# A fixed four-slot table for the feed-forward of a top-k attention kernel

## The chip, the core and the metric

The kernel runs on one core of one Trainium2 chip. The metric is device time in microseconds. The core has TensorE (PE, with its weight loads shown apart as PEld), VectorE (DVE), ScalarE (ACT), GpSimd (POOL) and SyncE (SP). Each takes its instructions in program order and waits where an operand or a buffer is not ready.

## The reference

Attention over 8 batches, 8 heads, 576 positions and 64 dimensions, in which a query keeps its 32 highest scores; then a feed-forward layer with a cosine gate. All in float32.

```python
scores = scale * np.matmul(q, k.transpose(0, 1, 3, 2))
kth = np.partition(scores, -top_k, axis=-1)[..., -top_k:-top_k + 1]
scores = np.where(scores >= kth, scores, -1e9)
scores = scores - np.max(scores, axis=-1, keepdims=True)
attn = np.exp(scores)
attn = attn / (np.sum(attn, axis=-1, keepdims=True) + 1e-09)
x = np.matmul(attn, v)          # to (4608 tokens, 512)
h = x @ w_in                    # 512 -> 2048
return (h * np.cos(h)) @ w_out  # 2048 -> 512
```

The second line from the end is why a product is gated with a sine: cos(h) is the sine of an argument that was first brought into range.

## The kernel before

**Units, slots, blocks.** The 4608 tokens are cut into 36 blocks of 128. A unit is 128 tokens with a pair of heads, so a block has four units and there are 144. One slot (`slot`, called for i = 0 to 143) handles three units at once at three stages: the top-k search of unit i, the mask and exponentials of unit i - 1, and the transfer of unit i - 2 through DRAM, which transposes its probabilities into a ring of five places. Four slots make a round and carry one block's worth of everything. Slots are named below by i modulo 4.

**Attention.** PE makes the scores of two units in every even slot (`scores`, L242). ACT copies them out (`take_scores`, L253 and L257). DVE folds 576 scores into two halves (L267) and takes the 32 highest with alternating MAX8 and MATCH_REPLACE8 (L359, L364); POOL makes the lower half `low` (`fold_sum` L283, `fold_low` L292), which DVE needs only in the last search round. A slot begins, on DVE, with the merge of the unit before (L347, L352); ACT then masks it (L378) and takes exponentials (L387). POOL splits the probabilities into 16-bit halves (L410) with their reciprocal sums (L412), and SP writes and transposes them. In every slot with i modulo 4 equal to 2, PE multiplies a block's probabilities by V (`values`, L475, into the PSUM tile `rim`), and DVE scales the result into `xT` (`take_values`, L491 or L499).

**Feed-forward.** A block's first product (`ff1`, L553) is made in four groups, each filling one PSUM bank of 128x512: mm0 to mm3 in this text. For each bank ACT makes two reads, `g` (L567) and `x` (L569, with a conversion to integers, `take_first`). For each pair of banks, 128x1024, POOL makes the argument in two operations (`reduce_first` L589, `reduce_second` L598), ACT takes the sine (L608, after a table load, and another load before the next exponentials), POOL multiplies (`gate`, L615). The second product (`ff2`, L628) runs over 16 slices; four make a group, o(0) to o(3), all in one bank, which ACT empties and stores (`take_second`, L638). The two banks of tag `mm` serve mm and o alike.

**The order.** Attention's order is written out in `slot`. The feed-forward is fed in by a planner: `plan` names for each slot of a round how many items of the two products are wanted at two or three places, and `can_first` and `can_second` decide by counters (gated tiles, ticks, loaded weights) whether an item may go. Filled banks wait in a list that `take_banks` empties; arguments, sines and gates go through queues. After the last slot `drain` and `forward` finish by the same queues with arguments and gates on DVE. q, k and v are loaded by SP inside `send`, at slots chosen by `load_at`. In the first twelve slots the weights are decoded by ACT, DVE and POOL between all this.

Of the kernel before, what the change touches and what calls it, by code (L numbers as in the profile page):

```python
# [17 lines left out]
P = 128  # L18
# [12 lines left out]
def kernel(  # L31
# [64 lines left out]
    ff = {"live": 0, "tick": 0, "now": 0, "end": False, "kind": 0, "half": 0, "open": 0, "late": False}  # L96
# [213 lines left out]
    def topk_first(u, w):  # L310

        u["top"] = tops[u["n"] % len(tops)]
        if w:
            merge_first(w)
        if u["n"] not in BUSY:
            fold_sum(u)
        fold_high(u)
        if w:
            merge_second(w)
        if u["n"] in BUSY:  # L320
            fold_now(u)
        topk_round(u, 0, [lambda: distances(w), lambda: None] if w else ())
# [82 lines left out]
    def split(u):  # L405


        s = u.pop("s").rearrange("p j k -> p (j k)").bitcast(U16)
        halves = work.tile([P, 2, 2 * S + P], U16, tag="halves", name="halves", bufs=1)
        nc.gpsimd.tensor_copy(out=halves[:, :, 0 : 2 * S], in_=s.rearrange("p (k h) -> p h k", h=2))  # L410
        rden = u.pop("rden").bitcast(U16).rearrange("p (j h) -> p h j", h=2)
        nc.gpsimd.tensor_copy(  # L412
            out=halves[:, :, 2 * S :].rearrange("p h (j d) -> p h j d", j=2),
            in_=rden.unsqueeze(3).to_broadcast([P, 2, 2, D]),
        )
        u["halves"] = halves
# [64 lines left out]
    def take_values(us):  # L481
# [23 lines left out]
        blk["left"] -= n  # L505
        blk["tick"] = ff["tick"]


    widths = [P] * (B * S // P)
    blocks, block_of = [], {}  # L510
    t0 = 0
    for w in widths:
        blk = {"t0": t0, "w": w, "left": 0, "g": [], "gated": []}
        for u in units:
            if t0 <= u["tok"] < t0 + w:
                block_of[u["tok"]] = blk
                blk["left"] += 1
        blocks.append(blk)
        t0 += w


    first = deque((blk, i) for blk in blocks for i in range(2 * NF * blk["w"] // 512))
    second = deque(
        (blk, i, f) for blk in blocks for i in range(blk["w"] // P) for f in range(0, NF, 2)
    )
    fresh = deque()
    waiting = deque()
    sined = deque()
    full = deque()

    def open_bank():

        if ff["open"] + len(full) == 2:
            take_banks()
        ff["open"] += 1

    def ff1(blk, i):
        w = blk["w"]
        nf = 256 // w
        part = i % 4  # L540
        if part == 0:
            blk["g"].append(ffw.tile([P, 1024], F32, tag="g", name="g", bufs=CHUNKS))
            blk["x"] = ffw.tile([P, 1024], F32, tag="x", name="x", bufs=XB)
            ff["live"] += 1
        if part % 2 == 0:
            open_bank()
            blk["mm"] = ps.tile([P, 512], F32, tag="mm", name="mm", bufs=2)
        g, mm = blk["g"][-1], blk["mm"]
        for a in range(nf):
            f = i * nf + a  # L550
            at = (part % 2 * nf + a) * w
            for c in range(NC):
                nc.tensor.matmul(  # L553
                    mm[:, at : at + w],
# [5 lines left out]
        if part % 2 == 0:  # L560
            return
        ff["open"] -= 1
        full.append((take_first, blk, g, blk["x"], mm, part // 2))

    def take_first(blk, g, x, mm, half):
        at = slice(half * 512, half * 512 + 512)
        nc.scalar.mul(out=g[:, at], in_=mm, mul=INV_2PI / UP)  # L567

        nc.scalar.activation(  # L569
            out=x[:, at].bitcast(I32), in_=mm, func=AF.Identity, bias=quarter, scale=INV_2PI / UP  # L570
        )
        if half == 1:
            fresh.append([blk, g, x, False, ff["now"] if ff["late"] else 0])

    def take_banks():
        while full:
            take, *what = full.popleft()
            take(*what)

    def reduce_first():  # L580

        if not fresh or (ff["late"] and not ff["end"] and fresh[0][4] == ff["now"]):
            return
        g, x = fresh[0][1:3]
        fresh[0][3] = True
# [5 lines left out]
        )  # L591

    def reduce_second():
        if not fresh or not fresh[0][3]:
            return
        blk, g, x, *_ = fresh.popleft()
        if not ff["end"]:
            nc.gpsimd.tensor_tensor(out=x, in0=g, in1=x, op=ALU.subtract)  # L598
        waiting.append((blk, g, x, ff["now"]))

    def sines(least):

        n = sum(c[3] < ff["now"] for c in waiting)
        if n == 0 or (n < least and waiting[0][3] + 2 > ff["now"]):
            return
        for _ in range(n):
            blk, g, x, _ = waiting.popleft()
            nc.scalar.activation(out=x, in_=x, func=AF.Sin, bias=halfpi, scale=TWO_PI_BELOW)  # L608
            sined.append((blk, g, x))

    def gate(n):
        for _ in range(min(n, len(sined))):
            blk, g, x = sined.popleft()
            eng = nc.vector if ff["end"] else nc.gpsimd
            eng.tensor_tensor(out=g, in0=g, in1=x, op=ALU.mult)  # L615
            blk["gated"].append(ff["tick"])

    def ff2(blk, i, f0):
        w = blk["w"]
        if f0 == 0:  # L620
            open_bank()
            blk["o"] = ps.tile([P, 512], F32, tag="mm", name="o2", bufs=2)
        o = blk["o"]
        per = 1024 // w
        for f in range(f0, f0 + 2):
            g = blk["g"][f // per]
            at = (f % per) * w + i * P
            nc.tensor.matmul(  # L628
                o, g[:, at : at + P], w_out[f], start=f == 0, stop=f == NF - 1
            )  # L630
        if f0 + 2 < NF:
            return
        ff["open"] -= 1
        full.append((take_second, blk, i, o))

    def take_second(blk, i, o):
        ob = ffw.tile([P, DM], F32, tag="ob", name="ob", bufs=1)
        nc.scalar.mul(out=ob, in_=o, mul=2.0 * math.pi / UP)  # L638
        row = blk["t0"] + i * P
        nc.scalar.dma_start(out=out[row : row + P, :], in_=ob)  # L640
        if i == blk["w"] // P - 1:
            ff["live"] -= len(blk["g"])
            blk["g"] = []

    def can_first():
        if not first:
            return False
        blk, i = first[0]
        if blk["left"] or ff["tick"] < blk["tick"] + 2 or wq["ready"] < (((i + 1) * (256 // blk["w"]) - 1) // FC + 1) * NC:
            return False  # L650
        return ff["now"] > NP + 2 and (i % 4 > 0 or ff["live"] + staged() < CHUNKS)

    def can_second():
        if not second or ff["now"] < 2 * NP + 3:
            return False
        blk, i, f = second[0]

        lag = 3 if ff["now"] < NU - NP else 2
        gated = sum(ff["tick"] >= t + lag for t in blk["gated"])
        return gated * 1024 // blk["w"] >= f + 2 and wq["ready"] >= NC * NF // FC + f + 2  # L660

    def item(kind):
        if not (can_first, can_second)[kind]():
            return False
        if kind == 0:
            ff1(*first.popleft())
        else:
            ff2(*second.popleft())
        return True

    def feed(*kinds):

        ff["tick"] += 1
        for kind in kinds:
            item(kind)

    def feed_any(n):

        ff["tick"] += 1
        for _ in range(n):  # L680
            kinds = (ff["kind"], 1 - ff["kind"])
            if second and second[0][2] == 0:
                kinds = (0, 1)
            if item(kinds[0]):
                kind = kinds[0]
            elif item(kinds[1]):
                kind = kinds[1]
            else:
                return
            if kind != ff["kind"] or ff["half"]:  # L690
                ff["kind"], ff["half"] = 1 - kind, 0
            else:
                ff["half"] = 1
# [19 lines left out]
    def load_at(i, *what):  # L713
        while i in at_slot or (what[0] is load_v and i % NP == 0):
# [23 lines left out]
    def send(x):  # L738

        split(x)  # L740
# [5 lines left out]
    plan = (  # L746
        ((0, 0), (1,), (1,)),
        ((0, 0), (1, 1), (0,)),
        ((0,), (1,), ()),
        ((1, 0, 0), (1, 1), ()),  # L750
    )

    def slot(i, u, w, x, z):
        n = (3, 4, 3, 4, 4, 3)[i] if i < NP + 2 else 2 if i != 2 * NP + 1 else 0
        if i < NP:
            for load, b, hp in at_once[i]:
                load(b, hp)
# [3 lines left out]
        ff["late"] = False  # L761
        topk_first(u, w)
# [18 lines left out]

        if i % 2:
            sines(1)
        if w:
            mask(w)
        if i % NP != 3:
# [114 lines left out]
```

## Time and profile before

| | us |
|---|---|
| median of 3 runs | 1413.0 (1412.85 to 1414.05) |
| profiled execution: span | 1410.6 |
| around that span, to the median | 2.4 |
| PE busy | 1354.6 (96%) |
| weight loads busy | 977.2 (69%) |
| DVE busy | 1336.9 (95%) |
| ACT busy | 1140.9 (81%) |
| POOL busy | 1165.3 (83%) |

The span runs from the first to the last instruction of the profiled execution; the runs time the whole execution. In an order of time each row gives the start in the span, the duration, the engine, the line, the operation and its tiles, and in brackets how long the engine had idled and what released it. In a table of groups the numbers behind the bar are the busy time in us, the mean in ns, and the idle time before. In a table of stretches the columns are sum and mean of the stretch, then busy time and count of PE, PEld, DVE, ACT and POOL, the granted TensorE clock, the share of the DMA engines, and GB/s. Durations of neighbours overlap a little, since operations are pipelined; the step from one start to the next is what a queue feels.

### The profile page before, as it was taken

To read this page: it belongs to the slowest core of one execution; us is meant where nothing else is said; L and a number is where in the kernel's file an instruction comes from. 1 tells how busy PE (TensorE), PEld (TensorE's weight loads), DVE (VectorE), ACT (ScalarE), POOL (GpSimd) and SP (SyncE) were. 2 spreads that over 40 slices of the span, in tenths; PEclk is the share of its full clock that TensorE was granted. 3 is DMA by queue.
4 is the path that set the end of the run, shared out by engine and by line. 5 is a ranking of instruction groups with operands and counts; after the bars stand their busy time and mean duration, and the time that the engine had idled before them with its cause. 6 is when DMAs were issued, how large, how long until landed. Compare 5 with 4: busy or idle time off the path is not lost.

```text
span 1410.6 us, 32284 instructions
## 1 busy us (share of the span) xinstructions
PE 1354.6 (96%) x11264; PEld 977.2 (69%) x11264; DVE 1336.9 (95%) x5004; ACT 1140.9 (81%) x2043; POOL 1165.3 (83%) x804
## 2 busy tenths in 40 slices
PE   5558999999999999999999999999999999999998
PEld 3445777777777777777777777777777777777775
DVE  7999999999999999999999999999999999999931
ACT  7887888888888888888888888888888888888831
POOL 4778988888888888888888888888888888898810
PEclk6788999999999999999999999999999999999999
DMA  9566776867675576668666576666766566655540
GB/s 291 193 196 181 204 178 169 203 172 196 162 177 152 161 199 159 181 160 197 174 170 159 152 181 187 170 170 160 207 165 165 158 174 166 148 157 146 152 101 15
DMA packets 427442, 240.12 MB, mean 170 GB/s; under 512 B 375952, under 2 KB 392592, under 8 KB 427280
## 3 DMA queue, kind: packets, MB, share of 16 engines
q1 hardware_dynamic: 420720, 224.22, 61.3%
q10 hardware_dynamic: 6560, 13.85, 2.8%
q8 instruction: 88, 1.44, 0.4%
q14 instruction: 74, 0.61, 0.1%
HBM read 45.09 MB, written 101.19 MB: 104 GB/s over the span
## 4 chain that ended last, share of the span: by engine, by line
PE 91%; DVE 7%; ACT 1%; DMA 0%; POOL 0%; issue 0%; SPq 0%; POOLq 0%
PE o L628 36%; PE mm L553 35%; PE rim L475 10%; PE sc L242 8%; DVE top L359 3%; PE rim L242 2%; DVE rest L364 2%; DVE low L364 1%; DVE rest L267 1%; DVE w_out L151 0%; DVE w_in L151 0%; DMA st<-in_moe_w_in_dram 0%; PE warm L844 0%; DVE low L275 0%; ACT s L387 0%; ACT s L378 0%
## 5 line engine op out<-in xcount | busy, mean ns | idle before, releaser
L553 PEld LDWEIGHTS mm<-xT,w_in 128*128 128x128 f32 x4608 | 537.9, 192 | 70.4 <-issue 65.5
L553 PE MATMUL mm<-xT,w_in 128*128 128x128 f32 x4608 | 539.2, 275 | 2.4 <-DVE xT L491 1.7
L628 PE MATMUL o<-w_out,g 128*128 128x512 f32 x1152 | 524.7, 599 | 0.0
L359 DVE MAX8 top<-rest 128x8 f32<-128x288 f32 x1152 | 479.0, 451 | 0.0
L364 DVE MATCH_REPLACE8 rest<-top,rest 128x288 f32<-128x288 f32 x864 | 376.7, 444 | 0.0
L628 PEld LDWEIGHTS o<-w_out,g 128*128 128x128 f32 x1152 | 207.7, 190 | 219.5 <-issue 214.8
L410 POOL COPY halves<-s 128x2304 uint16<-128x2304 uint16 x140 | 294.9, 2107 | 43.3 <-ACT s L387 40.1
L378 ACT ACTIVATE s<-s,top 128x576 f32<-128x576 f32 x288 | 207.6, 768 | 111.1 <-DVE top L352 99.0
L359 DVE MAX8 top<-low 128x8 f32<-128x288 f32 x576 | 241.8, 449 | 0.4 <-POOL low L292 0.4
L387 ACT ACTIVATE s<-s,nd 128x576 f32<-128x576 f32 x288 | 220.4, 769 | 1.1
L292 POOL TENSOR_TENSOR low<-low,rest 128x576 int32<-128x576 int32 x141 | 199.3, 1413 | 11.0
L283 POOL TENSOR_TENSOR low<-s 128x576 int32<-128x576 int32 x141 | 199.6, 1415 | 6.4 <-ACT s L259 6.4
L598 POOL TENSOR_TENSOR x<-g,x 128x1024 f32<-128x1024 f32 x68 | 161.2, 2370 | 5.7
L242 PE MATMUL sc<-k,q 64*64 64x448 f32 (+1 forms) x1120 | 145.6, 564 | 16.2 <-DVE low L275 9.8
L615 POOL TENSOR_TENSOR g<-g,x 128x1024 f32<-128x1024 f32 x68 | 161.0, 2367 | 0.0
L257 ACT COPY s<-rim 64x256 f32<-64x256 f32 (+1 forms) x280 | 103.1, 368 | 61.6 <-PE rim L475 60.0
L475 PE MATMUL rim<-ring,v 128*64 128x128 f32 (+1 forms) x2560 | 139.0, 268 | 0.0
L475 PEld LDWEIGHTS rim<-ring,v 128*64 128x64 f32 x2560 | 130.0, 139 | 6.5 <-issue 5.7
L253 ACT COPY s<-sc 128x896 f32<-128x896 f32 (+1 forms) x144 | 128.4, 892 | 3.3 <-PE sc L242 3.2
L567 ACT ACTIVATE g<-mm 128x512 f32<-128x512 f32 x144 | 85.2, 592 | 56.5 <-PE mm L553 55.5
L364 DVE MATCH_REPLACE8 low<-top,low 128x288 f32<-128x288 f32 x288 | 125.4, 443 | 0.0
L267 DVE TENSOR_TENSOR rest<-sc,s 128x576 f32<-128x576 f32 x144 | 107.7, 748 | 7.1 <-ACT s L259 6.6
(55 smaller groups left out, 1155.7 us busy)
## 6 DMA issues: line engine op xcount, KB each, us to landing
rows<-halves SPq DMA_DIRECT2D x140, 640.0 KB, 3.5
out_dram<-ob ACTq DMA_DIRECT2D x36, 256.0 KB, 2.1
q<-in_q_dram SPq DMA_DIRECT2D x31, 288.0 KB, 4.4
st<-in_moe_w_in_dram SPq DMA_DIRECT2D x16, 512.0 KB, 5.8
v<-in_v_dram SPq DMA_DIRECT2D x32, 256.0 KB, 4.2
k<-in_k_dram SPq DMA_DIRECT2D x31, 144.0 KB, 4.2
k<-in_k_dram SPq DMA_DIRECT2D x32, 128.0 KB, 4.5
st<-in_moe_w_out_dram SPq DMA_DIRECT2D x8, 512.0 KB, 5.1
```

The source lines that it names most:

```text
L242: nc.tensor.matmul(to[r0 : r0 + rows, rim_bank(r0, j) if k0 else place(u["hp"], j), 0 : k1 - k0], st["q"][d, q0 : q0 + rows], st["k"][d, k ...
L283: nc.gpsimd.tensor_tensor(out=u["low"].bitcast(I32), in0=s[:, :, 0:HS], in1=s[:, :, HS:S], op=ALU.add)
L292: nc.gpsimd.tensor_tensor(out=low, in0=low, in1=u["rest"][:, :, HS:S].bitcast(I32), op=ALU.subtract)
L359: nc.vector.max(to[:, j], src[:, j])
L364: nc.vector.match_replace(rest[:, j], to[:, j], src[:, j], NEG)
L378: nc.scalar.activation(out=s[:, j], in_=s[:, j], func=AF.Prelu, bias=less[:, j], scale=1.0, alpha=FAR)
L387: nc.scalar.activation(out=s[:, j], in_=s[:, j], func=AF.Exp, bias=nd[:, j : j + 1], scale=SCALE, accum_out=den[:, j, 0:1],)
L410: nc.gpsimd.tensor_copy(out=halves[:, :, 0 : 2 * S], in_=s.rearrange("p (k h) -> p h k", h=2))
L475: nc.tensor.matmul(to[d, r], lhsT, rhs, start=(bank, j) not in begun, stop=c == NT - 1 and u in us[-2:] and r0 + rows == P,)
L553: nc.tensor.matmul(mm[:, at : at + w], w_in[f // FC][:, c, (f % FC) * P : (f % FC + 1) * P], blk["xT"][:, c], start=c == 0, stop=c == NC - 1,)
L598: nc.gpsimd.tensor_tensor(out=x, in0=g, in1=x, op=ALU.subtract)
L628: nc.tensor.matmul(o, g[:, at : at + P], w_out[f], start=f == 0, stop=f == NF - 1)
```

## The change

The planner goes, with its counters and queues. `slot` names every feed-forward step for each of the four slots of a round, with the block counted as b = (i - 6) // 4. The groups keep their sizes. In program order a block's steps are: P@V and, at the end of slot 2, mm0; in slot 3, after the score copies, the reads of mm0, then mm1; in slot 0 the reads of mm1 between mask and exponentials, mm2, and at the end the first sine and the reads of mm2; in slot 1 mm3 and then o(0), which used to follow the next block's P@V and now stands ahead of it; o(1), o(2), o(3) in the following slots 2, 3 and 1. The store of a block stands in slot 1 between mask and exponentials.

Arguments and gates are made per bank, 128x512, and not per pair of banks: twelve POOL operations for a block and not six. They stand at named places, some of them ahead of `fold_sum` in a slot (`topk_first` takes a list for that). The sine stays at 128x1024. `split` becomes two functions that are called one after the other. `load_at` now keeps every load out of slots divisible by four, and so out of the sends of slot 1; before it kept only v out. `drain` is written out as one fixed list.

```diff
@@ -307,11 +307,13 @@
-    def topk_first(u, w):
+    def topk_first(u, w, ahead=()):
         u["top"] = tops[u["n"] % len(tops)]
         if w:
             merge_first(w)
+        for step in ahead:
+            step()
         if u["n"] not in BUSY:
             fold_sum(u)
         fold_high(u)
@@ -402,18 +404,21 @@
     def both(u):
         return [lambda: sums(u), lambda: reciprocal(u)] if u else ()
-    def split(u):
+    def split_scores(u):
         s = u.pop("s").rearrange("p j k -> p (j k)").bitcast(U16)
-        halves = work.tile([P, 2, 2 * S + P], U16, tag="halves", name="halves", bufs=1)
+        halves = u["halves"] = work.tile([P, 2, 2 * S + P], U16, tag="halves", name="halves", bufs=1)
         nc.gpsimd.tensor_copy(out=halves[:, :, 0 : 2 * S], in_=s.rearrange("p (k h) -> p h k", h=2))
+    def split_sums(u):
+        halves = u["halves"]
         rden = u.pop("rden").bitcast(U16).rearrange("p (j h) -> p h j", h=2)
         nc.gpsimd.tensor_copy(
             out=halves[:, :, 2 * S :].rearrange("p h (j d) -> p h j d", j=2),
             in_=rden.unsqueeze(3).to_broadcast([P, 2, 2, D]),
         )
-        u["halves"] = halves
...
+    def half_of(tiles, k):
+        return tiles[k // 2][:, k % 2 * 512 : k % 2 * 512 + 512]
...
+    def argument(b, k):
+        blk = block(b)
+        if blk is None:
+            return
+        g, x = half_of(blk["g"], k), half_of(blk["x"], k)
         if ff["end"]:
             nc.vector.tensor_tensor(out=x, in0=g, in1=x.bitcast(I32), op=ALU.subtract)
             return
         nc.gpsimd.tensor_scalar(
             out=x, in0=x.bitcast(I32), scalar1=1.0, scalar2=0.0, op0=ALU.mult, op1=ALU.add
         )
...
+        nc.gpsimd.tensor_tensor(out=x, in0=g, in1=x, op=ALU.subtract)
+    def sine(b, t):
+        blk = block(b)
+        if blk is None:
+            return
+        x = blk["x"][t]
+        nc.scalar.activation(out=x, in_=x, func=AF.Sin, bias=halfpi, scale=TWO_PI_BELOW)
+    def gate(b, k):
+        blk = block(b)
+        if blk is None:
+            return
+        g, x = half_of(blk["g"], k), half_of(blk["x"], k)
+        eng = nc.vector if ff["end"] else nc.gpsimd
+        eng.tensor_tensor(out=g, in0=g, in1=x, op=ALU.mult)
+    def second_run(b, r):
...
+        for f in range(r * PER, (r + 1) * PER):
+            g = half_of(blk["g"], f // PER)
...
@@ -711,7 +635,7 @@
     at_slot, at_once = {}, {}
     def load_at(i, *what):
-        while i in at_slot or (what[0] is load_v and i % NP == 0):
+        while i in at_slot or i % NP == 0:
             i += 1
         at_slot[i] = what
...
     def slot(i, u, w, x, z):
+        m, b = i % NP, (i - NP - 2) // NP
         n = (3, 4, 3, 4, 4, 3)[i] if i < NP + 2 else 2 if i != 2 * NP + 1 else 0
         if i < NP:
-            for load, b, hp in at_once[i]:
-                load(b, hp)
+            for load, bb, hp in at_once[i]:
+                load(bb, hp)
         load_weights(n, nc.sync if i < NP + 2 else nc.scalar)
         if x:
             (turn if i < NP + 2 else send)(x)
-        ff["late"] = False
-        topk_first(u, w)
+        if m == 1:
+            gate(b, 0)
+        elif m == 0:
+            argument(b, 0)
+        topk_first(u, w, [lambda: argument(b - 1, 3)] if m == 2 else ())
         fold_low(u)
         topk_round(u, 1)
         topk_round(u, 2)
         if i > 1:
             decode_second(NP)
             decode_third()
-        reduce_first()
-        reduce_second()
-        made = scored.get(i, [])
-        if z:
-            take_banks()
-        feed(*((0, 0) if i == NP + 2 else plan[i % NP][0]))
-        for m in made:
-            scores(m)
+        for o in scored.get(i, []):
+            scores(o)
         if z:
             values(z)
-        if i % 2:
-            sines(1)
+        if m == 1:
+            gate(b, 1)
+            argument(b, 2)
+            second_run(b - 1, 3)
+        elif m == 2:
+            second_run(b - 1, 1)
+        elif m == 3:
+            second_run(b - 1, 2)
         if w:
             mask(w)
-        if i % NP != 3:
-            take_banks()
+        if m == 0:
+            take_first(b, 1)
+            argument(b, 1)
+            first_bank(b, 2)
+        elif m == 1:
+            take_second(b - 1)
+            first_bank(b, 3)
+            second_run(b, 0)
         if w:
             exponentials(w)
-        take_banks()
+        if m == 2:
+            sine(b - 1, 1)
+            gate(b - 1, 2)
+            gate(b - 1, 3)
         if i + 1 < NU:
             take_scores(units[i + 1])
         def ahead():
             if z:
                 take_values(z)
@@ -801,43 +734,73 @@
         if i == 0:
             decode_second(NP)
             decode_third()
-        ff["late"] = True
-        gate(1)
-        feed(*plan[i % NP][1])
-        take_banks()
+        if m == 2:
+            first_bank(b, 0)
+        elif m == 3:
+            take_first(b, 0)
+            first_bank(b, 1)
+        elif m == 0:
+            sine(b, 0)
+            take_first(b, 2)
+        elif m == 1:
+            take_first(b, 3)
         decode_first(NP)
-        reduce_first()
-        reduce_second()
-        feed(*plan[i % NP][2])
...
+    def drain():
+        b = NB - 2
+        ff["end"] = True
+        w, x, last_two = units[NU - 1], units[NU - 2], units[NU - 2 :]
+        send(x)
+        merge_first(w)
+        merge_second(w)
+        distances(w)
+        mask(w)
+        take_first(b, 1)
+        argument(b, 0)
+        argument(b, 1)
+        first_bank(b, 2)
+        exponentials(w)
+        sums(w)
+        reciprocal(w)
+        sine(b, 0)
+        gate(b, 0)
+        gate(b, 1)
+        take_first(b, 2)
+        second_run(b - 1, 3)
+        first_bank(b, 3)
+        take_second(b - 1)
+        send(w)
+        second_run(b, 0)
+        argument(b, 2)
+        take_first(b, 3)
+        second_run(b, 1)
+        argument(b, 3)
+        sine(b, 1)
+        gate(b, 2)
+        gate(b, 3)
+        values(units[NU - 4 : NU - 2])
+        take_values(units[NU - 4 : NU - 2])
+        second_run(b, 2)
+        values(last_two)
+        take_values(last_two)
+        second_run(b, 3)
+        b += 1
+        first_bank(b, 0)
+        take_second(b - 1)
+        take_first(b, 0)
+        argument(b, 0)
+        for k in range(1, BANKS):
+            first_bank(b, k)
+            take_first(b, k)
+            argument(b, k)
+            if k % 2 == 1:
+                sine(b, k // 2)
+                gate(b, k - 1)
+                gate(b, k)
+        for r in range(BANKS):
+            second_run(b, r)
+        take_second(b)
...
     for i in range(NU):
-        ff["now"] += 1
-        wq["ready"] = wq["done"]
         u, w, x = (units[i - n] if n <= i else None for n in range(3))
-        z = valued.get(i)
-        slot(i, u, w, x, z)
-    ff["end"], ff["late"] = True, False
-    drain(units[NU - 1], units[NU - 2], units[NU - 4 : NU - 2])
-    drain(None, units[NU - 1], None)
-    drain(None, None, units[NU - 2 : NU])
-    while first or second or full:
-        forward(2)
+        slot(i, u, w, x, valued.get(i))
+    drain()
```

More of the change, by code (lines that the diff above doesn't have):

```diff
@@ L523 @@
[L523 to L533, printed above, removed]
-            take_banks()
[L535 to L541, printed above, removed]
+    for t0 in range(0, B * S, P):
+        blocks.append({"t0": t0})
+        block_of[t0] = blocks[-1]
@@ L559, in ff1, with take_first @@
                 )
-        if part % 2 == 0:
+    def take_first(b, k):
+        blk = block(b)
+        if blk is None:
             return
[L562 to L567, printed above, removed]
+        mm = blk["mm"].pop(k)
+        nc.scalar.mul(out=half_of(blk["g"], k), in_=mm, mul=INV_2PI / UP)
         nc.scalar.activation(
-            out=x[:, at].bitcast(I32), in_=mm, func=AF.Identity, bias=quarter, scale=INV_2PI / UP
+            out=half_of(blk["x"], k).bitcast(I32), in_=mm, func=AF.Identity, bias=quarter, scale=INV_2PI / UP
         )
[L572 to L582, printed above, removed]
+    def argument(b, k):
+        blk = block(b)
+        if blk is None:
             return
-        g, x = fresh[0][1:3]
-        fresh[0][3] = True
+        g, x = half_of(blk["g"], k), half_of(blk["x"], k)
         if ff["end"]:
@@ L591, in reduce_first @@
         )
-    def reduce_second():
-        if not fresh or not fresh[0][3]:
+        nc.gpsimd.tensor_tensor(out=x, in0=g, in1=x, op=ALU.subtract)
+    def sine(b, t):
+        blk = block(b)
+        if blk is None:
             return
[L596 to L604, printed above, removed]
-            return
[L606 to L609, printed above, removed]
@@ L640, in take_second @@
         nc.scalar.dma_start(out=out[row : row + P, :], in_=ob)
[L641 to L693, printed above, removed]
+        ff["live"] -= len(blk.pop("g"))
@@ L736, with send @@
         u["n"] = i
-    def send(x):
-        split(x)
+    def send(x, between=()):
+        split_scores(x)
+        split_sums(x)
+        for step in between:
+            step()
         write_halves(x)
```

107 lines of the change are left out of this document (29 added, 78 removed).

## The prediction

> **What bounds the kernel.** I read the page first, then the table of 100 us stretches, then the order of time of one round in the middle, engine by engine, and last the head and the tail.
>
> ```profile
> span 1410.6 us, 32284 instructions
> ```
>
> ```profile
> 700.00:800.00 100.00, 100.00 (x854) 72.05 (x853) 99.42 (x378) 83.60 (x152) 88.18 (x61) 1.00 0.61 163
> ```
>
> Mid-kernel PE is busy 100.00 of 100 us and DVE 99.42, at granted clock 1.00. Two engines are full; the steady stage offers a change at most DVE's missing half per cent. One round is four slots, DVE's L347 to L347. I call them by slot number modulo 4: slot 2 (P@V and xT), 3, 0, 1.
>
> ```profile
> 701.68 0.98 PE L242 MATMUL sc<-k,q 64*64 64x448 f32 x8
> ...
> 707.87 3.70 PE L628 MATMUL o<-w_out,g 128*128 128x512 f32 x8
> ...
> 718.41 3.73 PE L553 MATMUL mm<-xT,w_in 128*128 128x128 f32 x32
> 722.08 0.98 PE L242 MATMUL sc<-k,q 64*64 64x448 f32 x8
> ...
> 724.18 3.70 PE L628 MATMUL o<-w_out,g 128*128 128x512 f32 x8
> 727.71 3.73 PE L553 MATMUL mm<-xT,w_in 128*128 128x128 f32 x32
> 731.28 3.60 PE L628 MATMUL o<-w_out,g 128*128 128x512 f32 x8
> 734.72 3.73 PE L553 MATMUL mm<-xT,w_in 128*128 128x128 f32 x32
> 738.38 0.98 PE L242 MATMUL sc<-k,q 64*64 64x448 f32 x8
> ```
>
> Start to start, PE's round is 738.38 - 701.68 = 36.70 us without a hole: scores and P@V 6.19, o, mm and o 10.54, mm 3.67, scores 2.10, then 14.20 for o, mm, o, mm. DVE, meanwhile:
>
> ```profile
> 700.49 0.23 DVE L347 TENSOR_REDUCE top<-top 128x34 f32<-128x68 f32 x1
> ...
> 706.95 0.80 DVE L359 MAX8 top<-low 128x8 f32<-128x288 f32 x2
> ...
> 708.76 0.76 DVE L491 TENSOR_TENSOR xT<-rim,ring 128x256 f32<-128x256 f32 x2 [0.17 <-ACT s L257]
> ...
> 710.34 0.23 DVE L347 TENSOR_REDUCE top<-top 128x34 f32<-128x68 f32 x1
> ...
> 737.12 0.23 DVE L347 TENSOR_REDUCE top<-top 128x34 f32<-128x68 f32 x1
> ```
>
> DVE's one wait of the round is 0.17 us at xT, which follows P@V through the ACT copy of the score ends (L257), itself held until P@V is over. Without it DVE's round would be 36.5. So PE is the later engine by a hair, and its order around P@V sets the pace.
>
> **PE's order in a round.** The new table keeps the same work. From xT on: o(1), mm0, o(2), mm1, scores, mm2, o(3), mm3, o(0) of the block that these mm belong to, scores, P@V. The first half is unchanged in kind. The second has mm, o, mm, o for o, mm, o, mm: an o behind scores takes 3.53, one behind mm 3.44 (734.72 - 731.28); an mm ahead of scores 3.67, else 3.57. So 3.57 + 3.44 + 3.57 + 3.44 to 3.53 = 14.02 to 14.11 for 14.20; I take -0.13 per round (bounds 0 to -0.18).
>
> **mm1's wait, the largest term.** o holds one PSUM bank through the round, so mm0, mm1 and mm2 share the other: each waits for both ACT reads of the one before. Here the old planner emptied mm0's bank in slot 3 before `take_scores`; the table does it after, at the end of slot 3.
>
> ```profile
> 715.86 0.60 ACT L567 ACTIVATE g<-mm 128x512 f32<-128x512 f32 x1
> 716.36 0.68 ACT L569 ACTIVATE x<-mm,quarter 128x512 int32<-128x512 f32 x1
> 716.92 0.91 ACT L253 COPY s<-sc 128x896 f32<-128x896 f32 x1
> 717.71 0.75 ACT L257 COPY s<-rim 64x256 f32<-64x256 f32 x2
> ```
>
> Score copies from 715.86 take 1.54 (716.92 to 718.46), to 717.40; the second read then starts 0.50 on, lasts 0.68, and ends at 718.58. PE reaches mm1 at 718.41. One such wait exists already, in the first full round:
>
> ```profile
> 129.24 0.68 ACT L569 ACTIVATE x<-mm,quarter 128x512 int32<-128x512 f32 x1
> ```
>
> ```profile
> 129.98 3.84 PE L553 MATMUL mm<-xT,w_in 128*128 128x128 f32 x32 [0.65 <-ACT x L569]
> 133.75 0.98 PE L242 MATMUL sc<-k,q 64*64 64x448 f32 x8
> ```
>
> There PE started 0.06 after the read ended, and the group lasted 3.77 against 3.67: its first weight load is no longer hidden. So mm1 starts at 718.64 and PE comes out 0.23 + 0.10 = 0.33 late. This is a closed loop that DVE cannot absorb: P@V's end fixes xT, xT fixes slot 3 and its mask, exponentials and copies, and these fix mm1. Net +0.33 - 0.13 = +0.20 us per round. From slot 10 (DVE L347 at 109.24, below) to slot 142 there are 33 rounds; the first already had 0.65: 33 x 0.20 - 0.65 = +5.95. Bounds: no gap and the whole saving, 33 x -0.18 = -5.9; all of 0.33 plus another 0.10 for a late chain, 33 x 0.43 = +14.2.
>
> The Trainium skill (Perfetto Trace Analysis, Matmuls) says that independent matmul groups should rotate through PSUM banks, so that emptying one overlaps the next group. By that rule alone mm1, mm2 and mm3, all in one bank, would each show an emptying of 1.2, some 120 us in 33 rounds; the starts in the rows above, with the same single bank, show none, because other groups stand in between, and only where the reads come late is there a gap.
>
> The other bank waits are covered. mm2 has two score groups (2.10) between it and mm1, against 0.05 + 0.50 + 0.68 for the reads. o(0) waits for `take_second`, with mm3 (3.57) in between. The output DMA that `take_second` issues on ACT now stands ahead of slot 1's exponentials. P@V and its slot are where they were; q/k loads leave SP's slot-1 send, so the transposes that P@V needs have nothing new ahead of them.
>
> **ACT in slots 0 and 1**, where more is queued ahead of the score copies DVE needs.
>
> ```profile
> L378 ACT ACTIVATE s<-s,top 128x576 f32<-128x576 f32 x288 | 207.6, 768 | 111.1 <-DVE top L352 99.0
> ...
> L387 ACT ACTIVATE s<-s,nd 128x576 f32<-128x576 f32 x288 | 220.4, 769 | 1.1
> ...
> L608 ACT ACT_TABLE_LOAD x69 | 88.5, 1283 | 1.2
> ...
> L608 ACT ACTIVATE x<-x,halfpi 128x1024 f32<-128x1024 f32 x72 | 82.7, 1149 | 9.2 <-DVE x L587 6.3 <-POOL x L598 2.0
> ...
> L638 ACT ACTIVATE ob<-o 128x512 f32<-128x512 f32 x36 | 21.5, 597 | 15.4 <-PE o L628 14.6
> ```
>
> mm1 ends at 722.41. Then two reads 1.06 (715.86 to 716.92), exponentials 1.53 (220.4/144), copies 1.54, table 1.28 and sine 1.15: 729.0. Two reads 1.06, mask 1.44, the store with its issue about 1.0 (estimate, from 0.60 plus an issue), table 1.28, exponentials 1.53, copies 1.54: 736.9. DVE wants them at 737.12 + 0.15. Slack 0.4: no stall, and xT's wait would swallow 0.3 more.
>
> **POOL by halves.**
>
> ```profile
> L410 POOL COPY halves<-s 128x2304 uint16<-128x2304 uint16 x140 | 294.9, 2107 | 43.3 <-ACT s L387 40.1
> ...
> L292 POOL TENSOR_TENSOR low<-low,rest 128x576 int32<-128x576 int32 x141 | 199.3, 1413 | 11.0
> ...
> L598 POOL TENSOR_TENSOR x<-g,x 128x1024 f32<-128x1024 f32 x68 | 161.2, 2370 | 5.7
> ...
> L589 POOL TENSOR_SCALAR x<-x 128x1024 f32<-128x1024 int32 x68 | 71.3, 1049 | 26.1 <-ACT x L569 26.0
> ```
>
> ```profile
> 719.36 0.40 POOL L412 COPY halves<-rden 128x256 uint16<-128x256 uint16 x1 [1.27 <-DVE rden L400]
> ```
>
> A half of 512 lies between 2370/2 = 1.19 and the 576-wide 1.41; a line through 576 and 1024 gives 1.28, less some overlap 1.22. The conversion: about 0.53 to 0.7, with its hand-over 0.61. From 719.36 POOL has, to slot 2's `fold_low`: three split sums at 0.36, two splits at 2.05, four argument halves at 1.83, two gates at 1.22, three fold pairs at 2.89 (twice 1.41 and a hand-over): 1.08 + 4.10 + 7.32 + 2.44 + 8.67 = 23.6, plus 0.4 waiting for the sine that ends at 729.0: 743.4. DVE wants `low` 6.46 us into the slot (706.95 - 700.49): 743.58. Just in time; a lateness up to 0.4 only replaces xT's wait. Cost nothing; cover 0.5 us.
>
> **Head.** o(0) of block 0 moves into slot 9, where PE idles:
>
> ```profile
> 107.57 0.70 PE L242 MATMUL rim<-k,q 64*64 64x128 f32 x8 [5.70 <-ACT s L257]
> ```
>
> ```profile
> 96.11 2.56 POOL L160 TENSOR_TENSOR w_out<-w_out,st 128x512 int32<-128x512 int32 x2 [1.76 <-ACT s L257]
> ```
>
> ```profile
> 95.66 0.70 ACT L133 ACTIVATE w_out<-st 128x512 f32<-128x512 f32 x1
> ...
> 99.37 1.15 ACT L608 ACTIVATE x<-x,halfpi 128x1024 f32<-128x1024 f32 x1
> ...
> 106.78 0.74 ACT L257 COPY s<-rim 64x256 f32<-64x256 f32 x2
> ```
>
> ```profile
> 109.24 0.23 DVE L347 TENSOR_REDUCE top<-top 128x34 f32<-128x68 f32 x1
> ```
>
> But the first sine now needs the second argument half, which POOL does behind the decode: 96.11 + 2.56 + 1.83 = 100.5, not 99.37. Behind the sine stand two weight decodes (some 2.4, from 95.66 to the table load) that were ahead of it. The copies that ended at 107.52 end 1.1 + 2.4 later, at 111.0, and DVE wants them at 109.39. DVE and then P@V come +1.5 later (bounds 0 and 3).
>
> **Tail.** After the last P@V of the slots one o of 3.5 less is left: the gain of the early group appears here, at the end, not in the rounds. Against it, mm1 of slot 143 starts later, by 0.23 and by up to 0.98 more, since slot 142 has one score group less in front of PE but ACT comes no sooner: I take 0.9, and 0.10 for the load. And mm2 behind it has no scores for cover: 0.05 + 0.50 + 0.68 + 0.06 idle, 0.10 for the load. -3.5 + 1.0 + 1.4 = -1.1 (bounds -3.5 and 0). The last block's gates keep ahead: after mm3 two o groups (6.9) cover reads, argument, sine and gate, which now sit on ACT and an idle DVE.
>
> **Sum.** +5.95 + 1.5 - 1.1 = +6.35 us on the profiled execution, whose span is 1410.6. The median of the runs, 1413.0, lies 2.4 above that span, for what lies around it; I add the same: 1419.4.
>
> **Rivals.** *The gap costs nothing.* If PE has hidden slack, or ACT gets through slot 3 0.3 us sooner, rounds stay at 36.70 or lose the 0.13: 0 to -4.3; head and first round +1.5 - 0.65; tail -1.4, with no lag to carry: -0.55 to -4.85, so 1408.2 to 1412.5, middle 1410.3. For it: the busy PE of the page is modelled. Against it: DVE's 99.42% leaves 0.2 us per round, about what xT waits here. The Trainium skill (same page, Identifying the Most-Contended Engine) judges TensorE by its weight loads, not its matmuls; at 72% it would have room, and this rival would hold. The starts above, with no hole, speak the other way.
>
> *POOL becomes late, much slower.* If a half tensor_tensor costs the 576-wide 1.41 and the conversion 0.7, four of the former and two of the latter in the chain since the sine add 4 x 0.19 + 2 x 0.17 = 1.1; past the 0.5 of cover DVE loses 0.6 per round, 33 x 0.6 = 20 on top of the forecast: 1439. It decides from a half of about 1.35 us. For it: 88% busy before, and 12 short pieces for 6 long ones per round. Against: 1.28 by the two rows.
>
> **Chances.** Forecast 0.6 (own range 1414 to 1426), no cost 0.26, POOL 0.14. A measurement tells 0.2%, 2.8 us. Faster takes most of the second case, 0.18; the rest of it and the forecast's low end are within 0.2%, 0.14; slower 0.68. The range 1408 to 1431 holds the forecast, nearly all of the second case and the mild part of the third.
>
> **What would show it.** Right: mm1 idle about 0.25 us per round on the ACT read L558, rounds of 36.9, DVE's wait at xT near 0.4, a DVE wait near 110 us of 1.5, no DVE wait on `low`. Wrong: PE without holes, or `low <- POOL` among DVE's waits.

## The result, and the profile after

| | median | runs | ratio to before |
|---|---|---|---|
| before | 1412.92 us | 1411.18 to 1414.05, 4 runs | |
| after | 1458.45 us | 1457.03 to 1459.99, 4 runs | 1.0322, 95% interval 1.0307 to 1.0337 |
| forecast | 1419.4 us | range 1408 to 1431 | |

The change makes the kernel 45.5 us slower. The direction was forecast, the size was not: the time lies 27 us above the range.

The page of the changed kernel: its span, PE's first product and scores, and POOL's new halves (columns as before: busy us, mean ns of one | idle time before, and what ended most of it).

```profile
span 1455.0 us, 32398 instructions
...
L542 PE MATMUL mm<-xT,w_in 128*128 128x128 f32 x4608 | 546.1, 277 | 7.8 <-ACT x L558 6.6
...
L591 POOL TENSOR_TENSOR g<-g,x 128x512 f32<-128x512 f32 x136 | 172.0, 1275 | 22.4 <-ACT x L582 18.7
L242 PE MATMUL sc<-k,q 64*64 64x448 f32 (+1 forms) x1120 | 156.4, 578 | 35.7 <-DMA k<-in_k_dram 21.1
L574 POOL TENSOR_TENSOR x<-g,x 128x512 f32<-128x512 f32 x136 | 173.9, 1279 | 11.3
```

A releaser of 21 us stands there that the forecast never named: the scores wait for k from memory. The waits of PE and of DVE (us in total, times, longest) say that they are few and long:

```profile
PE sc L242 <- DMA k<-in_k_dram: 21.1, 5, 5.2
...
PE mm L542 <- ACT x L558: 6.6, 21, 1.4
```

```profile
DVE xT L496 <- ACT s L257: 36.3, 25, 9.3
...
DVE top L361 <- POOL low L292: 1.8, 5, 0.9
```

Two stretches of 100 us, the second with such a wait in it (busy us of PE, its weight loads, DVE, ACT, POOL, then PE's granted clock):

```profile
700.00:800.00 100.00, 99.42 (x787) 69.61 (x789) 99.00 (x376) 84.47 (x153) 89.08 (x76) 1.00 0.66 173
500.00:600.00 100.00, 94.41 (x809) 67.98 (x808) 89.66 (x341) 74.23 (x134) 80.06 (x68) 0.97 0.63 163
```

**An ordinary round** (PE in order of time):

```profile
686.78 0.98 PE L242 MATMUL sc<-k,q 64*64 64x448 f32 x8
...
692.96 3.70 PE L603 MATMUL o<-w_out,g 128*128 128x512 f32 x8
...
700.07 3.60 PE L603 MATMUL o<-w_out,g 128*128 128x512 f32 x8
703.88 3.84 PE L542 MATMUL mm<-xT,w_in 128*128 128x128 f32 x32 [0.21 <-ACT x L558]
707.65 0.98 PE L242 MATMUL sc<-k,q 64*64 64x448 f32 x8
...
709.75 3.84 PE L542 MATMUL mm<-xT,w_in 128*128 128x128 f32 x32
...
723.96 0.61 PE L242 MATMUL sc<-k,q 64*64 64x448 f32 x4
```

It lasts 723.96 - 686.78 = 37.18 us. From o(1) to the scores behind mm1 it takes 707.65 - 692.96 = 14.69 where the kernel before took 14.21 (707.87 to 722.08); from mm2 to the next scores 14.21, where before took 14.20. So the whole loss of the round is at mm1, and the second half gained nothing.

**A long round.** Between the starts of slot 54 and slot 58 (L349, DVE's first operation of a slot, L347 in the kernel before) lie 45.9 us. SP, PE and DVE in slot 54, and PE's clock (last but two column) around it:

```profile
529.17 0.34 SPq L446 DMA_DIRECT2D rows<-halves  x1
529.61 0.38 SPq L199 DMA_DIRECT2D q<-in_q_dram  x1
530.04 0.92 SPq L205 DMA_DIRECT2D k<-in_k_dram  x1
...
531.66 0.59 SPq L203 DMA_DIRECT2D k<-in_k_dram  x1
```

```profile
528.98 0.97 PE L242 MATMUL sc<-k,q 64*64 64x448 f32 x4
534.96 1.47 PE L242 MATMUL sc<-k,q 64*64 64x448 f32 x2 [5.00 <-DMA k<-in_k_dram]
...
543.98 3.70 PE L603 MATMUL o<-w_out,g 128*128 128x512 f32 x8
```

```profile
544.87 0.76 DVE L496 TENSOR_TENSOR xT<-rim,ring 128x256 f32<-128x256 f32 x2 [9.23 <-ACT s L257]
```

```profile
529.00:535.00 6.00, 0.99 (x6) 0.25 (x6) 5.93 (x23) 5.15 (x9) 5.49 (x6) 0.88 0.74 229
535.00:537.00 2.00, 2.00 (x16) 1.68 (x20) 0.64 (x3) 0.00 (x0) 2.00 (x3) 0.50 1.23 262
537.00:539.00 2.00, 2.00 (x22) 1.62 (x20) 0.00 (x0) 0.91 (x1) 1.83 (x1) 0.50 0.01 2
...
541.00:544.00 3.00, 3.00 (x57) 2.83 (x53) 0.00 (x0) 0.00 (x0) 0.00 (x0) 1.00 0.03 5
```

The k that PE wants at 529.9 is sent for at 530.0 to 531.7. PE waits 5.00 us, runs on at half its clock for some 5 us, and reaches o(1) 15.0 us after the scores began (543.98 - 528.98), where an ordinary round takes 6.18. DVE, with xT as the next thing it needs, stands for 9.23 us. In the kernel before the same load left in slot 53:

```profile
508.58 0.34 SPq L441 DMA_DIRECT2D rows<-halves  x1
509.02 1.43 SPq L199 DMA_DIRECT2D q<-in_q_dram  x1
...
511.68 0.60 SPq L203 DMA_DIRECT2D k<-in_k_dram  x1
```

This follows from one condition of the diff. `load_at` files a load under a slot, and it goes out in the send of the slot after. The kernel before kept only v loads from numbers divisible by 4, that is out of slot 1's send; the change keeps q and k loads out too. Followed through the code, many loads move by a slot. Most q and k loads that move keep four slots or more in hand; four keep none. These were filed under 16, 52, 88 and 124 and move to 17, 53, 89 and 125: those of the last head pair of batches 1, 3, 5 and 7. They leave in the sends of slots 18, 54, 90 and 126, and scores in these very slots read them. Their buffers come free too late to file them sooner.

The rounds from these four slots last 44.52, 45.93, 45.00 and 45.97 us; the same rounds before lasted 36.52, 36.63, 36.83 and 36.70. The other 27 rounds between slots 18 and 142 are 0.42 longer each, 11.4 in all. That accounts for the 44.4 us between the two spans:

| part | us |
|---|---|
| late loads: 34.7 in four rounds, less 4 x 0.42 | +33.1 |
| 31 rounds x 0.42 | +13.1 |
| up to slot 18: +0.5, and -0.9 because slot 1 starts that much sooner in this profile | -0.4 |
| slots 142 to 144 and the end | -1.4 |

### The profile page after: what moved, and what is told of

Its sections match the earlier page's. It is cut to its first block, busy times and chain, and to the rows that moved or that the text cites. A ratio compares the mean times of both kernels' runs of the same rounds, so it can differ in the third digit from the quotient of the medians.

```text
span 1455.0 us, 32398 instructions
## 1 busy us (share of the span) xinstructions
PE 1376.2 (95%) x11264; PEld 977.9 (67%) x11264; DVE 1342.4 (92%) x5012; ACT 1144.9 (79%) x2043; POOL 1197.3 (82%) x1008
## 4 chain that ended last, share of the span: by engine, by line
PE 63%; ACT 20%; DVE 11%; POOL 2%; issue 1%; DMA 1%; SPq 0%; ACTq 0%; DVEq 0%; POOLq 0%
PE mm L542 26%; PE o L603 18%; PE rim L480 9%; PE sc L242 8%; ACT s L389 4%; DVE top L361 4%; ACT s L380 4%; ACT L389 3%; ACT s L257 3%; ACT s L253 2%; PE rim L242 2%; DVE rest L267 2%; ACT g L556 1%; ACT x L558 1%; DVE rest L366 1%
## 5 line engine op out<-in xcount | busy, mean ns | idle before, releaser
L542 PEld LDWEIGHTS mm<-xT,w_in 128*128 128x128 f32 x4608 | 532.6, 192 | 75.1 <-issue 38.5
L542 PE MATMUL mm<-xT,w_in 128*128 128x128 f32 x4608 | 546.1, 277 | 7.8 <-ACT x L558 6.6
L591 POOL TENSOR_TENSOR g<-g,x 128x512 f32<-128x512 f32 x136 | 172.0, 1275 | 22.4 <-ACT x L582 18.7
L242 PE MATMUL sc<-k,q 64*64 64x448 f32 (+1 forms) x1120 | 156.4, 578 | 35.7 <-DMA k<-in_k_dram 21.1
L574 POOL TENSOR_TENSOR x<-g,x 128x512 f32<-128x512 f32 x136 | 173.9, 1279 | 11.3
L418 POOL COPY halves<-rden 128x256 uint16<-128x256 uint16 x140 | 56.5, 403 | 70.6 <-DVE rden L402 70.6
```

What stands on the lines that cost most here:

```text
L242: nc.tensor.matmul(to[r0 : r0 + rows, rim_bank(r0, j) if k0 else place(u["hp"], j), 0 : k1 - k0], st["q"][d, q0 : q0 + rows], st["k"][d, k ...
L542: nc.tensor.matmul(mm[:, a * P : (a + 1) * P], w_in[f // FC][:, c, (f % FC) * P : (f % FC + 1) * P], blk["xT"][:, c], start=c == 0, stop=c ...
```

## The experiments

Two theories: A, the late k loads make the four long rounds; B, the sends come late for another reason (halves on POOL, the early group). For the 0.42 us: C, mm1's wait for the bank; D, the order of mm and o, or POOL.

**Load condition taken back (e1).**

```diff
-        while i in at_slot or i % NP == 0:
+        while i in at_slot or (what[0] is load_v and i % NP == 0):
```

> The changed kernel with one line taken back: q and k loads may again start in the send of every slot, so the last q/k load ahead of a two-batch block goes out one slot earlier. Theory A (the k loads of slots 18, 54, 90 and 126 miss their scores): in the changed kernel these four rounds last 44.52, 45.93, 45.00 and 45.97 us where the others last 37.1; without the lateness they last 37.1 to 37.7, so 33 us come back: 1425 us (1422 to 1428), no wait of PE on k. Theory B (the sends themselves are late because of the halves on POOL or the early o group, and the load line matters little): within 5 us of 1458. Under A what is left over the kernel before, 12 us, is 0.42 us in each of 31 rounds.

1424.95 us, ratio 1.0097 (1.0082 to 1.0112). The four rounds last 37.17, 37.11, 37.18 and 37.05, the rest as in the changed kernel. 33.5 us come back: A.

**The condition alone (e2)**, put into the kernel before, the reverse of the diff above.

> The kernel before with that one line alone as the changed kernel has it. Theory A: the same four k loads come one slot later and PE waits for each as it does in the changed kernel: 1413 + 33 = 1446 us (1440 to 1450), four long rounds of about 45 us, all others as before. Theory B (the stall needs the new table): 1413 to 1418.

1444.74 us, ratio 1.0233 (1.0218 to 1.0249): rounds of 45.57, 44.73, 44.30 and 43.88 from the four slots, all other rounds from slot 14 on within 0.02 of before. The stall needs nothing of the new table. It costs 32.7 here and 33.5 there.

**Loads ahead of the rows' write (e3)**, in the changed kernel.

```diff
-        write_halves(x)
         for load, b, hp in at_send.pop(x["n"] + 2, ()):
             load(b, hp)
+        write_halves(x)
         transposes(x)
```

> The changed kernel, load line untouched, but in each send the loads are issued ahead of the rows' write instead of behind it, so that they don't wait for POOL's split. In slot 54 SP is free from 525.1 and the rows' write went out at 529.2: the loads go 4.4 us sooner, and PE's wait of 5.00 for k shrinks to 0.6. If only the wait counts, each of the four rounds gets back 4.4 of its 8 to 9 us, 18 us in all: 1441. If, as the rows say (granted clock 0.50 for about 4 us behind the wait, and scores and P@V 9.0 us instead of 6.2), the low clock after an idle PE is a second price that a wait of 0.6 does not call up, each gets back 7 us or more: 1428 to 1431. Theory B: no change.

1430.12 us, ratio 1.0131 (1.0116 to 1.0147). Slot 54 starts 3.0 us earlier than in the changed kernel. Its SP, PE and clock:

```profile
522.27 0.52 SPq L199 DMA_DIRECT2D q<-in_q_dram  x1
...
526.21 0.34 SPq L446 DMA_DIRECT2D rows<-halves  x1
```

```profile
526.01 1.77 PE L242 MATMUL sc<-k,q 64*64 64x448 f32 x7
...
533.36 3.70 PE L603 MATMUL o<-w_out,g 128*128 128x512 f32 x8
```

```profile
526.00:528.00 2.00, 2.00 (x21) 1.02 (x21) 2.00 (x9) 1.97 (x6) 1.92 (x3) 1.00 0.55 222
```

The load goes out 3.9 us ahead of the rows, no wait of the products is marked, and the clock stays at 1.00. The time is that of the expectation in which a low clock is a second price beside the wait. Still, scores and P@V take 7.35 us for 6.18, and each of the four rounds is 1.2 to 1.3 us longer than in e1. The weight loads of the same scores show what holds them:

```profile
526.68 0.19 PEld L242 LDWEIGHTS sc<-k,q 64*64 64x64 f32 x2 [0.47 <-DMA k<-in_k_dram]
527.20 0.13 PEld L242 LDWEIGHTS sc<-k,q 64*64 64x64 f32 x1 [0.33 <-DMA k<-in_k_dram]
```

They wait 0.80 us for k, which is still a little late. How the rest of the 1.2 comes about is open.

**Bank read first (e4, and e7 again)**: e1, and the reads of mm0's bank ahead of slot 3's score copies.

```diff
+        if m == 3:
+            take_first(b, 0)
         if i + 1 < NU:
             take_scores(units[i + 1])
...
         elif m == 3:
-            take_first(b, 0)
             first_bank(b, 1)
```

> The kernel with the loads as before and, besides, the reads of mm0's bank on ACT in slot 3 put ahead of the score copies again. Theory C (the 0.42 us that every round has over the old one are mm1's wait for these reads, 0.37, and its exposed first weight load, 0.10, with nothing gained in the second half of the round): rounds of 36.7, 31 x 0.42 = 13 us less than with the loads alone: 1412 us (1409 to 1415). Theory D (the order of mm and o in the second half, or POOL's halves, hold the round at 37.1): 1425, unchanged, with the wait moved elsewhere.

> The kernel with loads as before and the bank read first once more, beside the two above, on the same chip: 1410.4 us, 0.9989 of the kernel before; 1409 to 1412.

1410.42 us, ratio 0.9989 (0.9979 to 0.9999), and again 1410.16, ratio 0.9988 (0.9979 to 0.9997). Rounds are those of the kernel before (36.55 to 36.84 from slot 34 on, apart from batch boundaries), mm1 starts 3.44 behind o, and 14.5 us are gone: C. This is the fastest of the kernels run, ahead of before by 0.1%, less than the 0.2% that the prediction took a measurement to tell.

**Early group undone (e5)**, from e4: o(0) to o(3) in slots 2, 3, 0 and 1.

```diff
         elif m == 2:
-            second_run(b - 1, 1)
+            second_run(b - 1, 0)
         elif m == 3:
-            second_run(b - 1, 2)
+            second_run(b - 1, 1)
+        elif m == 0:
+            second_run(b - 1, 2)
...
             first_bank(b, 3)
-            second_run(b, 0)
...
+        second_run(b - 1, 2)
```

(The last line stands in `drain`.)

> The kernel with loads as before and the bank read first, and now also the early group undone: o(0) behind P@V again, o(1) in slot 3, o(2) in slot 0, o(3) in slot 1. Theory A (the early group is worth only what it saves behind the last P@V; the steps of mm and o come to 14.22 us on either side of the scores in both orders): rounds stay at 36.70 and the 2.0 us that the stretch from the last slot to the end was shorter (64.6 for 66.6) come back: 1412.4 us (1411 to 1414). Theory B (the early group fills a hole of PE in each round): 0.1 to 0.2 us per round, 1414 to 1418. Theory C (it costs, because P@V comes 3.5 us later behind the scores): 1406 to 1409.

1474.91 us, ratio 1.0448 (1.0433 to 1.0462): none of the three. Rounds last 38.5 to 38.6. ACT and DVE at the end of one slot 1:

```profile
764.88 0.60 ACT L613 ACTIVATE ob<-o 128x512 f32<-128x512 f32 x1 [0.84 <-PE o L603]
```

```profile
768.84 0.16 DVE L397 TENSOR_REDUCE den<-dens 128x2 f32<-128x4 f32 x1 [1.06 <-ACT s L389]
```

The table stores o ahead of the exponentials. Without the early group, o(3) is not finished there: ACT waits, and with it the exponentials that DVE wants.

**The store late (e8)**, from e5: `take_second(b - 1)` from ahead of slot 1's exponentials to behind its score copies.

> The kernel with the early group undone (1474.9 us), and the store of o moved from ahead of slot 1's exponentials to behind its score copies, where the kernel before had it. Theory A (the 64.7 us that undoing the early group cost are ACT's wait for o(3) in front of the exponentials, 0.84 a round, which makes den and the score copies late by 1.06 and 0.65; the early group is worth just the place of the store, and the end): rounds back at 36.70, the end 2.0 us longer than with the early group: 1412.4 us (1410 to 1415). Theory B (without the early group PE's order itself starves the scores, in front of which it now waits 0.96 and 0.34): 1450 to 1475.

1446.78 us, ratio 1.0246 (1.0231 to 1.026). 28 us come back, not all: rounds of 37.7 to 37.8. POOL and DVE in slot 2:

```profile
718.94 0.62 POOL L571 TENSOR_SCALAR x<-x 128x512 f32<-128x512 int32 x1 [1.03 <-ACT x L558]
```

```profile
723.82 0.82 DVE L361 MAX8 top<-low 128x8 f32<-128x288 f32 x2 [0.75 <-POOL low L292]
```

mm3 too ends one group later, so its read comes late for the argument that stands ahead of the folds on POOL, and `low` is late. That this is the rest of the loss is read from the trace and not tested by a further kernel.

**Whole tiles (e6)**, from e4: arguments and gates of the slots by 1024. `whole` makes the two operations of an argument, or the one of a gate, on such a tile.

```diff
-        if m == 1:
-            gate(b, 0)
-        elif m == 0:
-            argument(b, 0)
-        topk_first(u, w, [lambda: argument(b - 1, 3)] if m == 2 else ())
+        if m == 1:
+            whole(gate, b, 0)
+        topk_first(u, w, [lambda: whole(argument, b - 1, 1)] if m == 2 else ())
...
-            gate(b, 1)
-            argument(b, 2)
...
-            argument(b, 1)
+            whole(argument, b, 0)
...
-            gate(b - 1, 2)
-            gate(b - 1, 3)
+            whole(gate, b - 1, 1)
```

> The kernel with loads as before and the bank read first, with arguments and gates of the slots by whole tiles of 1024 in the same table: the argument of a tile where its second half stood, the gate where its first (in slot 1) or last (in slot 2) half stood. Theory A (POOL in slot 2 has nothing to spare: fold_low comes 0.16 us late already with a half in front of it): the whole argument is 1.5 us longer (1.05 + 2.37 for 0.62 + 1.28), DVE waits 1.4 us on low in each round, 0.2 of it instead of xT's wait: 33 x 1.2 = 40 us, 1450 (1435 to 1460). Theory B (POOL's idle time absorbs it, since four whole pieces take 0.8 us less in all than eight halves): 1409 to 1413.

1415.29 us, ratio 1.002 (1.0011 to 1.003): 5.1 above e7, not 40. POOL and DVE around slot 2, which starts at 703.05 (in e7 at 699.64):

```profile
700.90 2.10 POOL L412 COPY halves<-s 128x2304 uint16<-128x2304 uint16 x1 [0.73 <-ACT s L389]
...
703.56 1.05 POOL L602 TENSOR_SCALAR x<-x 128x1024 f32<-128x1024 int32 x1
```

```profile
709.97 0.82 DVE L361 MAX8 top<-low 128x8 f32<-128x288 f32 x2 [0.38 <-POOL low L292]
```

```profile
698.64 2.10 POOL L412 COPY halves<-s 128x2304 uint16<-128x2304 uint16 x1
```

The last row is e7's. The split starts 2.15 us ahead of the slot here and 1.00 there, where the half argument of slot 1 still runs in front of it. So the whole tile is 1.5 longer behind the split, but the split comes 1.15 sooner: `low` is 0.38 late. My expectation had counted the piece that grew and not the one that left.

**q behind the rows (e9)**: the changed kernel with k ahead of the rows' write and q behind it, for a wait of middling length.

> The changed kernel with its late loads, k issued ahead of the rows' write and q behind it: a wait of PE between the 5.0 us of the changed kernel and the none that was left with all loads ahead. In slot 54 q goes out at 529.6 as before, k some 5 us sooner; landing about 4.3 us after the issue (the median of these loads), q frees the scores at 533.9: a wait of 4.0. If the low clock follows any long wait, the granted clock behind it is 0.50 and a round loses 4.0 + 2.8 + 1: four rounds at about 7.8, 1456 us. If it needs a wait near 5 us, the clock stays at 1.00 and a round loses 4 to 5: 1442 to 1446.

1446.79 us, ratio 1.0245 (1.0229 to 1.0262), between the two cases, because both occur in the profiled execution. That one took 1448.92, the other three 1446.73 to 1446.80; how often the clock fell in those is not on record. PE and its clock in slots 90 and 126:

```profile
874.35 1.01 PE L244 MATMUL sc<-k,q 64*64 64x448 f32 x2 [3.52 <-DMA q<-in_q_dram]
...
1215.94 0.59 PE L244 MATMUL sc<-k,q 64*64 64x448 f32 x2 [3.51 <-DMA q<-in_q_dram]
```

```profile
875.00:877.00 2.00, 2.00 (x22) 1.46 (x16) 1.48 (x6) 0.90 (x2) 1.87 (x2) 0.50 1.08 225
...
1217.00:1219.00 2.00, 2.00 (x43) 1.62 (x36) 1.11 (x5) 0.86 (x1) 2.00 (x2) 1.00 2.04 254
```

And the wait of slot 90 itself in two stretches, both without a matmul, at a granted clock of 1.00 and then 0.50:

```profile
870.83:872.72 1.89, 0.00 (x0) 0.00 (x0) 1.89 (x8) 1.84 (x7) 1.89 (x2) 1.00 1.06 344
872.72:874.35 1.63, 0.00 (x1) 0.04 (x1) 1.63 (x8) 1.62 (x2) 1.55 (x2) 0.50 0.50 184
```

The waits of the four slots are alike, 3.46 to 3.52 us. In slots 18, 54 and 90 the clock fell, and the rounds last 43.21, 44.19 and 44.14; in slot 126 it did not, and the round lasts 41.51. The expectation had put the low clock at 2.8 us a round; by these rounds it is worth 1.6 to 2.6 (last section).

## Why the size was wrong

**The step that failed** is the sentence "q/k loads leave SP's slot-1 send, so the transposes that P@V needs have nothing new ahead of them". It asks what the move takes out of the way of others and not when the moved loads are themselves due. Worth 0 in the sum, it costs 33.1, three quarters of the loss. The rows that would have told stood in the trace of before: the load of slot 53 above is issued by 512.3 and lands at 514.9, and its scores run at 517.62 (first row of PE in slot 54 there), 5.3 us behind the issue, against a move by one slot, 8.93. None of the rivals covered it either.

```profile
517.62 0.98 PE L242 MATMUL sc<-k,q 64*64 64x448 f32 x8
```

**mm1's wait** was right in place and kind: idle 0.21 on L558, the group at 3.77, and e4 removes it with two lines put back in their old place. The size was 0.33 and is 0.48 in the round shown: mm1 starts 3.81 behind o (703.88 - 700.07) where e7 has 3.44, so 0.37 for the 0.23 of the sum, and 0.10 for the weight load as priced. The rival in which the gap costs nothing is out: the rounds became longer by all of it.

**The saving of 0.13 in the second half** did not come: 14.21 for 14.20. I had priced an mm behind scores at 3.57, like one behind o; it takes 713.43 - 709.75 = 3.68.

```profile
713.43 3.60 PE L603 MATMUL o<-w_out,g 128*128 128x512 f32 x8
```

So a round loses 0.42 on average, at the upper bound of 0.43 that the forecast gave, and the 31 rounds 13.1. With the loads as before, the change would have cost 12.9 us (e1, 1424.95 for 1412.09): within the range, and about twice the 6.35 of the sum.

**POOL by halves** was right: 1275 and 1279 ns for the 1.22 to 1.28 expected. Any wait of DVE on `low` was named as a sign against the forecast; there are five, 1.8 us in all, and behind the first 160 us only two of 0.16. The rival "POOL becomes late" is out, and e6 shows that whole tiles would cost 5.1 in this table.

**The head** was read right and summed wrongly. DVE's new waits near 110 us come to 0.78 + 0.65 = 1.43, for 1.5:

```profile
108.62 0.16 DVE L397 TENSOR_REDUCE den<-dens 128x2 f32<-128x4 f32 x1 [0.78 <-ACT s L389]
110.05 0.76 DVE L267 TENSOR_TENSOR rest<-sc,s 128x576 f32<-128x576 f32 x1 [0.65 <-ACT s L257]
```

```profile
119.52 0.49 DVE L499 TENSOR_TENSOR xT<-rim,ring 128x128 f32<-128x128 f32 x2 [1.54 <-ACT s L257]
```

But the kernel before (second fence) stood 1.54 at the xT right behind, and that wait is gone. Slot 18 starts 0.5 us later than before if both are counted from the start of slot 1; the forecast, with two rounds in it, gives 1.5 + 0.4 - 0.65 = 1.25.

**The end** is near: -1.4 for -1.1 from slot 142 on. Of its parts one is shown alone, the bare wait of mm2 that was worked out as 0.05 + 0.50 + 0.68 + 0.06 = 1.29:

```profile
1393.70 3.84 PE L542 MATMUL mm<-xT,w_in 128*128 128x128 f32 x32 [1.27 <-ACT x L558]
```

**The early group** was costed as a matter of 3.5 us at the end. e5 and e8 show more: in this table it is what makes o(3) ready where ACT's fixed order asks for it, and, as the trace of e8 reads, mm3 too. Taken out alone it costs 64.8 us against e7, and with the store late as well still 36.6.

## What to carry to other kernels

A moved transfer has two prices: what it was in the way of, and its own due time. Before a load is put at nothing, look up its first reader, and compare the slack in the old trace, from the landing to that reader, with the step by which it moves. Four slots of 144 made three quarters of this loss. In a table written by hand, places depend on each other: undo one alone and the loss can be larger than all that the change moved.

## What the runs showed of the hardware

A wait of PE costs more than its length. Behind 5.0 us without matmuls the granted clock was 0.50 for some 5 us, and the 5.00 of slot 54 became 8.8 of delay at o(1). With a wait of 3.5 us the clock fell in three cases of four. Against the rounds of e1, the wait costs 4.5 us where the clock stayed at 1.00 (slot 126 alone) and 6.0 to 7.1 where it fell, so the low clock itself is worth 1.6 to 2.6.

The Trainium skill (TensorE: Matmul & The Clock Gate, Part 1: The HAM clock gate) says that the clock halves after an idle window of about 3.4 us, that about as much sustained work brings it back, and that the window runs freely, whatever the kernel does. The free run agrees: by the clock record of the changed kernel's trace the falls of slots 18, 54, 90 and 126 come at 192.24, 533.57, 878.32 and 1219.65 us, which is 100, 101 and 100 steps of 3.41 us apart, and the low clock lasts one such step or two.

That the window must be idle from end to end is not borne out. In slot 90 of e9 the clock fell 1.89 us after PE had stopped (the two rows of the wait above). In slot 18 of e9 it fell at 193.47, 1.4 us after PE had begun again at 192.09. In the 3.41 us before the three falls of e9 PE was idle for 1.9 to 2.1 us. In slot 126 the same wait lay across two steps, with 1.6 and 1.9 idle in them, and the clock stayed. So the place of a wait in these steps decides along with its length, and by these few cases the limit is near 1.9 of 3.41 us; this is an estimate, since the ends of PE's work are modelled. The waits of 4.6 to 5.2 us in the changed kernel all brought the clock down, and PE worked at the low clock for some 3 us in slot 18 and 5 in slot 54.
